# Linear attention and an ELU feed-forward on one core: nine neighbouring tokens per partition for q, whole slots of k and v in the first batch, and feed-forward columns written in token order

## The chip, the cores and the metric

The kernel runs on one core of one Trainium2 chip. The metric is the device time of one execution in microseconds (us). The engines are PE (TensorE, matmuls), DVE (VectorE), ACT (ScalarE), POOL (GpSimd) and SP (SyncE, which here only issues transfers). They run side by side and wait for each other through semaphores.

## What is computed

For each of 8 batches and 8 heads, with 576 tokens and 64 channels: q is normalised by a softmax over its channels, k by a softmax over the tokens, `kv` is a 64x64 matrix per head, and the attention output is `q_s @ kv`. The heads side by side give 4608 rows of 512, which go through a feed-forward network of width 2048 with an ELU between.

```python
q_s = softmax(q, axis=-1)                 # over 64 channels
k_s = softmax(k, axis=2)                  # over 576 tokens
kv  = einsum('bhsd,bhde->...', k_s, v)    # [b, h, 64, 64]
x   = (q_s @ kv).transpose(0, 2, 1, 3).reshape(4608, 512)
h   = x @ w_in                            # [4608, 2048]
g   = where(h > 0, h, exp(min(h, 0)) - 1)
out = g @ w_out                           # [4608, 512]
```

All inputs and the output are float32; q, k and v are 9.4 MB each, the two weights 4.2 MB each.

## The kernel before

A batch's 576 tokens are split into 512 (`SM`, four rows `R` on each of 128 partitions) and a rest of 64 (`SR`). The feed-forward of batch `j` runs in 16 steps (`NCH`), one per 128 columns of the hidden layer. A step has four matmuls into one PSUM bank (`hidden`, line 778), an exponential on ACT (766), a `min`-like step on POOL (767) and the combination on DVE (`elu`, 789), which writes the hidden tile GT. Three steps later (`LAG`) four matmuls (`project`, 799) multiply that GT tile by `w_out` and accumulate in four output banks. The rests of all 8 batches are kept in XTR and go through the network as a ninth round of 16 steps at the end.

While batch `j` is in the feed-forward, the attention of batch `j + 1` is prepared by the same engines. The order is written out by hand in tables of words: `FIRST` for the steps of batch 0, `SECOND` for batch 1, `LATER` for the others. Each step has three strings: words that come after the hidden matmuls, after the project matmuls, and after the elu. `do` turns each word into instructions. The first batch has its own list, `START`, since nothing runs beside it, and `AT` gives its PSUM banks.

The words that matter:

- `load`: transfers of q, k or v, issued on SP's queue in the order of the words. A, B and M are the first four heads, the last four, or all, for the 512 tokens; R is the rest, in two transfers of 64 partitions. `w1` and `w2` load weights on POOL's queue. `hold` lets SP wait for the last hidden matmul.
- `qmax`, `qsub`, `qexp`, `qsum`, `qmul`: softmax of q, into QS (and `qmulr` for the rest, into QSR). A suffix names the engine, with gp for POOL.
- `turn` and `wide`: a DMA transpose of QS into QW and a copy into QT, where channels lie on partitions; `pturn` and `pwide` do it with PE instead.
- `kmax`, `kturn`, `kacross`, `diag`, `kspread`, `copy`: the maximum of k over tokens, for batches 0 and 1. `peak`, `join`, `kout`, `kin` do the same for later batches with a transposing reduction and a small transfer through memory. Then `ksub`, `kexp`; `kraw`, `kmin` do the subtraction with PE in the first batch.
- `vconv`, `kv`, `kfac`: v in bfloat16, the kv matmuls and their normalisation into MB.
- `att` and `xc`, or `flat` and `xflat`: the matmul of MB and QT, and the copy into XT, the input of the feed-forward. `rest0`, `rcopy0` and `xrest` serve the rest.

An engine carries out its instructions in the order of the program. Where an instruction waits, all behind it on that engine waits too. The elu and the store of the output read:

```python
self.op("dve", lambda: v.scalar_tensor_tensor(self.GT[n % NG][:, :], ps, 0.0, ES[:, :],
                                              ALU.max, ALU.min),
...
rows = self.out[j * S:j * S + SM, :].rearrange("(p r) c -> r p c", r=R)[t]
```

Of the kernel before, what the change touches and what calls it, by code (L numbers as in the profile page):

```python
# [17 lines left out]
SR = S - SM  # L18
CUTS = (0, 320, 832, 1344, 1856, 2304)
# [15 lines left out]
AT = {"rawA": 0, "rawA2": 1, "rawB": 3, "rawB2": 2, "rawS": 7, "rawT": 4,  # L35
      "kturnA": 5, "kturnB": 3, "kvA": 5, "kvB": 6, "pturnA": 6, "pturnB": 4,
      "att0": 5, "att1": 7, "att2": 3, "att3": 6}
START = ("load:K:0:A load:Q:0:A load:K:0:R kmax:A qmax:A load:K:0:B kmax:S kraw:A load:Q:0:B kraw:S "
         "kmax:B kmax:T qsub:A:gp qmax:3 warm:4:3 kturn:A load:K:1:R kacross:A load:V:0:A w1:2:4 "
         "w1:0:2 qexp:A kturn:B load:V:0:R diag:act:A w2:0:2 kmin:S kacross:B kexp:S kraw:T w1:4:6 "  # L40
         "qsub:3:gp vconv:R:gp qmax:2 qsum:A diag:dve:B qsub:2:gp qmul:A:dve qexp:3 w2:2:5 kmin:A "
         "qsum:3 load:V:0:B qexp:2 kraw:B kmin:T pturn:A w1:6:8 vconv:A:gp qmul:3:gp kexp:A "
         "load:K:1:M pwide:A:act await:sp:QS0 qsum:2 kv:A kfac:A:dve kmin:B att:0 qmul:2:gp "
         "load:Q:1:A kexp:T att:1 w1:8:10 load:Q:0:R vconv:B:dve pturn:B kexp:B xc:0 kv:B xc:1:dve "
         "kfac:B:dve w2:5:6 load:Q:1:R h:2:4 pwide:B:act att:2 att:3 xc:2 h:0:2 kmax2:B w1:10:12 "
         "xc:3 kmax2:A kmax2:R ")
FIRST = {
    0: ("", "", ""),
    1: ("", "", ""),
    2: ("qmax:A", "w2:6:8", ""),  # L50
    3: ("qsub:0 w1:12:14", "qsub:1:dve", ""),
    4: ("", "qmax0:R qexp:A w2:8:12", "qsum:A load:Q:1:B qsub0:R"),
    5: ("", "kturn kacross", "qexp0:R qmul:A qsum0:R"),
    6: ("diag", "qmax:C", ""),
    7: ("qsub:D:dve", "kspread qsub:2 w1:14:16", "hold copy load:V:1:RAB"),
    8: ("qexp:C", "qmulr0:gp ksub:1:dve", "ksub:0:dve load:K:2:MR"),
    9: ("pturn:A", "ksub:3 ksub:R", "qsum:C pwide:A:act"),
    10: ("qmul:B:dve pturn0:R kexp:A", "pwide0:R:act", ""),
    11: ("vconv:A:dve", "rest0 w2:12:13 vconv:R", "ksub:2:dve rcopy0:act"),
    12: ("load:Q:2:ABR pturn:B kexp:R vconv:B:gp", "", "load:V:2:MR pwide:B:act"),  # L60
    13: ("kv:A", "kexp:B kfac:A:dve att:0", "xc:0 w2:13:15 w2:15:16 peak2:A"),
    14: ("kv:B kfac:B:dve", "att:1 qmulr:dve peak2:B", "xc:1"),
    15: ("peak2:R join2 att:3 xc:3", "", "turn:R att:2 xc:2 kout2"),
}
SECOND = {
    0: ("qmax:A", "qsub:0:dve qmax:C", "load:Q:2:MR qsub:1"),
    1: ("qexp:A", "qsub:D", ""),
    2: ("qsub:2", "", ""),
    3: ("kin qsum:A", "qmul:0", "qexp:C wide0:R:act"),
    4: ("", "qsum:C", "qmul:1:dve ksub:2:dve"),  # L70
    5: ("", "load:K:2:MR", ""),
    6: ("qmulr:dve ksub:R:dve", "kexp:R qmul:B:dve", "ksub:3:dve"),
    7: ("rest0 turn:A", "rcopy0:dve", "vconv:B"),
    8: ("", "vconv:R ksub:A", "kexp:B peak2:B"),
    9: ("peak2:R kexp:A", "vconv:A:dve", "turn:R peak2:A"),
    10: ("", "", "turn:B join2"),
    11: ("", "kv:AB", "wide:A:gp"),
    12: ("kfac:AB:dve", "load:K:3:MR wide:R:act", ""),
    13: ("wide:B:gp", "flat:0", "xflat:0:act"),
    14: ("flat:1", "load:V:2:MR xflat:1:dve flat:2", "xflat:2:act"),  # L80
    15: ("kout2 flat:3", "xflat:3:dve", "flat:4 xflat:4:act xrest:act qmax2:A"),
}
LATER = {
    0: ("qsub:0", "", ""),
    1: ("", "kin qsub:1:dve", "vconv:R"),
    2: ("qsub:2", "", ""),
    3: ("qexp:A", "ksub:R:dve ksub:0:dve", "qsum:A"),
    4: ("", "", "qsub:D ksub:1:dve"),
    5: ("", "ksub:3:dve ksub:2:dve", "qexp:C"),
    6: ("", "kexp:A qmul:A:dve", "qsum:C"),  # L90
    7: ("kexp:B", "vconv:A:gp", ""),
    8: ("vconv:B turn:A kexp:R", "qmulr:gp", ""),
    9: ("", "peak2:A kv:AB qmul:B kfac:AB:dve", "wide:A:act peak2:R"),
    10: ("", "", "load:K:3:MR"),
    11: ("flat:0 xflat:0:act turn:R", "wide:R:act", "qmax2:A"),
    12: ("peak2:B join2", "turn:B", "flat:1 xflat:1:act wide:B:gp"),
    13: ("load:Q:3:MR", "flat:2", "qmax2:C xflat:2:act"),
    14: ("", "flat:3", "load:V:2:MR kout2 xflat:3:act"),
    15: ("flat:4", "", "xflat:4:act xrest:dve"),
}  # L100
CHANGED = {
    0: ("", "", "qmax:C qsub:0"),
    2: ("", "", "qsub:2 load:Q:2:MR"),
}
TABLES = {0: FIRST, 1: SECOND, 2: {**LATER, **CHANGED}}
NONE = ("", "", "")


class Ev:

    __slots__ = ("sem", "val", "know")

    def __init__(self, sem, val, know):
        self.sem, self.val, self.know = sem, val, know


class Gen:
# [103 lines left out]
    def init(self):  # L221
# [8 lines left out]
        for f in range(4):  # L230
            op("gp", lambda: g.memset(self.MB[f][:, :, :].bitcast(F32), 0.0), (), [f"MB{f}"])
# [803 lines left out]
```

## Time and profile before

| | us |
|---|---|
| runs shown (2) | 313.07 and 314.11, median 313.59 |
| profiled execution, whole | 312.28 |
| its span in the profile | 310.5 |
| PE, DVE, ACT, POOL busy | 296.0, 243.8, 177.9, 174.0 |
| elu: each of 144 on DVE | 0.679 |
| subtraction in k, 128x512, on DVE / POOL | 0.745 / 1.727 |
| q's multiply, 128x1024, on DVE / POOL | 1.215 / 1.906 |
| transfers | 51.63 MB, mean 166 GB/s |

The span runs from the first to the last instruction that the profile shows; about 1.8 us of the profiled execution lie around it. Busy times are of one execution. In group lines, the columns are line, engine, operation, output and input tile, shapes, count, then the busy time in us and the mean of one in ns, then the idle time before them and what ended it. An instruction can start before the one ahead of it has quite ended, so sums of means are slightly above the busy time of a window.

### The profile page before, as it was taken

Reading aid. Unit: us, or ns where it says so; the run is one execution under the profiler, and the core shown is the slowest. Engines: PE = TensorE matmul, PEld = TensorE weight load, DVE = VectorE, ACT = ScalarE, POOL = GpSimd, SP = SyncE. Lnnn points to the kernel's source line nnn. Section 1 sums busy time; section 2 is a strip of 40 time slices with the busy share of each in tenths; the row PEclk is TensorE's granted clock in tenths of the full one; section 3 lists DMA queues with packets and bytes.
Section 4 is the critical chain, followed back from the end, with each engine's and each line's share of the span. In section 5 each row is a group of like instructions: output and inputs, shape, how many; then the busy total and the mean of one; then the engine's idle time right before and its main releaser. Section 6 shows DMA issues by size and latency. Waiting matters only on the chain.

```text
span 310.5 us, 4547 instructions
## 1 busy us (share of the span) xinstructions
PE 296.0 (95%) x1601; PEld 236.0 (76%) x1601; DVE 243.8 (79%) x420; ACT 177.9 (57%) x295; POOL 174.0 (56%) x229
## 2 busy tenths in 40 slices
PE   3688999999999999999999999999999999999995
PEld 1356876688778868887887888888888888888884
DVE  6999998999879997999799979997895354335541
ACT  1475786558357845694478556955695543334432
POOL 2987985655636843675467636763676333333330
PEclk9999999999999999999999999999999999999999
DMA  7999999998918695439742974152412030003003
GB/s 234 320 352 328 373 338 312 294 320 146 290 41 246 165 255 167 170 60 268 208 170 48 266 223 169 34 129 70 169 34 44 0 137 0 0 2 136 0 1 135
DMA packets 65607, 51.63 MB, mean 166 GB/s; under 512 B 29360, under 2 KB 58288, under 8 KB 65584
## 3 DMA queue, kind: packets, MB, share of 16 engines
q1 hardware_dynamic: 57984, 41.23, 49.4%
q0 software_dynamic: 6400, 8.39, 10.0%
q10 hardware_dynamic: 1200, 1.72, 1.8%
q8 instruction: 12, 0.20, 0.3%
q14 instruction: 11, 0.09, 0.1%
HBM read 38.27 MB, written 9.45 MB: 154 GB/s over the span
## 4 chain that ended last, share of the span: by engine, by line
PE 80%; DMA 8%; DVE 6%; ACT 2%; POOL 1%; SPq 1%; issue 1%; DVEq 0%
PE bank L778 38%; PE bank L799 38%; DMA QWR<-QSR 4%; DMA W2S<-in_moe_w_out_dram 3%; PE bank L709 2%; DMA KR<-in_k_dram 2%; DVE QZ L604 1%; ACT ES L766 1%; PE bank L535 1%; POOL ES L767 1%; DVE GT L789 1%; DVE QS L618 1%; SPq L276 1%; PE bank L652 1%; DVE KA L299 0%
## 5 line engine op out<-in xcount | busy, mean ns | idle before, releaser
L767 POOL TENSOR_SCALAR ES<-ES 128x512 f32<-128x512 f32 x144 | 95.7, 666 | 119.2 <-ACT ES L766 118.8
L799 PE MATMUL bank<-W2S,GT 128*128 128x512 f32 x576 | 154.5, 392 | 1.2 <-DVE GT L789 0.9
L778 PE MATMUL bank<-XT,W1S 128*128 128x512 f32 x512 | 139.2, 394 | 0.2 <-ACT XT L696 0.2
L789 DVE SCALAR_TENSOR_TENSOR GT<-bank,ES 128x512 fp32r<-128x512 f32 x144 | 96.8, 679 | 50.9 <-PE bank L778 42.0
L766 ACT ACTIVATE ES<-bank 128x512 f32<-128x512 f32 x144 | 85.6, 597 | 87.2 <-PE bank L778 86.4
L799 PEld LDWEIGHTS bank<-W2S,GT 128*128 128x128 f32 x576 | 107.2, 188 | 24.0 <-DVE GT L789 1.4
L778 PEld LDWEIGHTS bank<-XT,W1S 128*128 128x128 f32 x512 | 94.1, 188 | 19.7 <-ACT XT L696 0.9
L594 POOL TENSOR_TENSOR QR<-QR,QM 128x512 f32<-128x512 f32 (+3 forms) x24 | 28.7, 1199 | 5.4 <-DVE QM L586 5.2
L600 ACT ACTIVATE QR<-QR 128x1024 f32<-128x1024 f32 (+3 forms) x18 | 19.0, 1060 | 11.6 <-POOL QR L594 10.2
L586 DVE TENSOR_REDUCE QM<-QR 128x16 f32<-128x1024 f32 (+3 forms) x18 | 21.7, 1208 | 0.5 <-DMA QR<-in_q_dram 0.5
L604 DVE TENSOR_REDUCE QZ<-QR 128x16 f32<-128x1024 f32 (+3 forms) x18 | 21.7, 1206 | 0.0
L731 ACT ACTIVATE XT<-bank 128x512 fp32r<-128x512 f32 (+2 forms) x28 | 15.4, 552 | 10.1 <-PE bank L709 9.9
L414 DVE TENSOR_TENSOR KR<-KR,NB 128x512 f32<-128x512 f32 x25 | 17.8, 745 | 0.3
L778 PE MATMUL bank<-XTR,W1S 128*128 128x512 f32 x64 | 16.6, 389 | 0.0
L452 ACT ACTIVATE EK<-KR 128x1024 bf16<-128x1024 f32 x14 | 14.7, 1050 | 0.8 <-POOL KR L414 0.8
L618 POOL TENSOR_TENSOR QS<-QR,QI 128x1024 f16<-128x1024 f32 (+1 forms) x9 | 14.5, 1617 | 1.1 <-DVE QI L606 1.1
L367 DVE TRANSPOSE_TENSOR_REDUCE KM<-KR 128x32 f32<-128x1024 f32 x12 | 14.8, 1237 | 0.4 <-DMA KR<-in_k_dram 0.4
L778 PEld LDWEIGHTS bank<-XTR,W1S 128*128 128x128 f32 x64 | 12.0, 188 | 2.5
L709 PE MATMUL bank<-QT,MB 128*128 128x320 f32 (+5 forms) x48 | 11.8, 306 | 0.8 <-ACT QT L731 0.7
L709 PEld LDWEIGHTS bank<-QT,MB 128*128 128x128 f32 x48 | 8.5, 188 | 5.0 <-ACT QT L731 1.7
L618 DVE TENSOR_TENSOR QS<-QR,QI 128x1024 f16<-128x1024 f32 (+1 forms) x9 | 10.5, 1170 | 0.1
L809 DVE COPY OSB<-bank 128x512 f32<-128x512 f32 x16 | 10.3, 686 | 0.4 <-PE bank L799 0.3
(96 smaller groups left out, 204.9 us busy)
## 6 DMA issues: line engine op xcount, KB each, us to landing
out_dram<-OSB SPq DMA_DIRECT2D x35, 256.0 KB, 2.8
KR<-in_k_dram SPq DMA_DIRECT2D x7, 1024.0 KB, 6.0
VR<-in_v_dram SPq DMA_DIRECT2D x6, 1024.0 KB, 7.4
QR<-in_q_dram SPq DMA_DIRECT2D x5, 1024.0 KB, 7.2
W1S<-in_moe_w_in_dram POOLq DMA_DIRECT2D x8, 512.0 KB, 11.3
QR<-in_q_dram SPq DMA_DIRECT2D x6, 512.0 KB, 8.2
VR<-in_v_dram SPq DMA_DIRECT2D x4, 512.0 KB, 7.7
W2S<-in_moe_w_out_dram POOLq DMA_DIRECT2D x3, 512.0 KB, 10.4
```

The source lines that it names most:

```text
L414: self.op(en, lambda: e.tensor_tensor(kv, kv, m, ALU.subtract), keys + ["NB"], keys)
L586: self.op("dve", lambda: v.tensor_reduce(self.QM[:, g], QR[:, g, :], AX.X, ALU.max), self.qkeys(b, part), self.qstat("QM", part))
L594: self.op(en, lambda: e.tensor_tensor(QR[:, g, :], QR[:, g, :], m, ALU.subtract), keys + self.qstat("QM", part), keys)
L600: self.op("act", lambda: a.activation(QR[:, g, :], QR[:, g, :], AF.Exp), keys, keys)
L604: self.op("dve", lambda: v.tensor_reduce(self.QZ[:, g], QR[:, g, :], AX.X, ALU.add), self.qkeys(b, part), self.qstat("QZ", part))
L618: self.op(en, lambda: e.tensor_tensor(out, src, z, ALU.mult), keys + self.qstat("QI", part), [f"QS{x}" for x in cells])
L709: last = pe.matmul(self.bank[bank][:, a - c0:b - c0], self.MB[f][:, :, :].rearrange("p u d -> p (u d)"), self.QT[:, f, a - f * S:b - f * S ...
L766: self.op("act", lambda: a.activation(ES[:, :], ps, AF.Exp), [f"bank{bank}"], [ek])
L767: self.op("gp", lambda: g.tensor_scalar(ES[:, :], ES[:, :], -1.0, 1.0, ALU.add, ALU.mult), [ek], [ek])
L778: return pe.matmul(ps, self.W1S[:, kc, c * 128:(c + 1) * 128], x[:, kc, 0:SM], start=(kc == 0), stop=(kc == 3))
L789: self.op("dve", lambda: v.scalar_tensor_tensor(self.GT[n % NG][:, :], ps, 0.0, ES[:, :], ALU.max, ALU.min), [f"bank{bank}", ek], [f"GT{n ...
L799: return pe.matmul(self.bank[OB[t]][:, :], self.GT[n % NG][:, t * 128:(t + 1) * 128], self.W2S[:, c, :], start=(c == 0), stop=(c == NCH - 1))
```

## The change

Three layouts change, and with them the order tables.

- **q**: each partition holds nine neighbouring tokens of four head slots, so the 512 and the rest are one piece. Partitions 0 to 63 hold two heads of a half and 64 to 127 the other two. A batch's q comes in four transfers of 64 partitions with runs of 2304 bytes. The softmax runs on 18 groups of 64 per half. Two DMA transposes of nine blocks replace two of eight and one of two. XT's columns are then ordered by row within the nine first, and by partition second.
- **k and v of the first batch**: loaded as slots of two neighbouring heads, 128 partitions with 2304 bytes in a run. The maximum is one reduction over the nine rows; `kv_first` does 72 matmuls with 64 partitions each, in place of 40.
- **elu and store**: GT is written in token order, which is a step of 8 elements within a row; an output tile then holds 16 groups of 8 neighbouring rows, and its store goes to 16 runs of 16 KB. The ninth round is unchanged in its elu.

For batch 1 the maxima of k are found by `peak` and `join`, so `kturn`, `kspread` and `copy` go. The words of `START`, `FIRST`, `SECOND` and `LATER` are put in a new order, with other engines for some of them.

```diff
-LATER = {
-    3: ("qexp:A", "ksub:R:dve ksub:0:dve", "qsum:A"),
-    5: ("", "ksub:3:dve ksub:2:dve", "qexp:C"),
-    6: ("", "kexp:A qmul:A:dve", "qsum:C"),
...
+LATER = {
+    4: ("ksub:0:dve qexp:B", "ksub:3", "vconv:B"),
+    6: ("qsum:B vconv:A", "ksub:2 qmul:A", "turn:A kexp:R kexp:A"),
+    7: ("", "kexp:B peak2:B", "qmul:B"),
+    9: ("qmax2:A", "vconv:R", "turn:B wide:A:gp"),
...
+START = ("load:K:0:1 load:K:0:0 load:Q:0:1 kmax:A load:Q:0:0 load:K:0:3 qmax:A kraw:A load:K:0:2 "
+         "kraw:T kturn:A qsub:A:gp w1:2:4 load:Q:0:2 load:Q:0:3 kmax:B qmax:2 load:V:0:3 kacross:A "
+         "load:V:0:2 kturn:B qexp:A kacross:B load:Q:1:0 qmax:3 qsub:2:gp diag:dve:A qsub:3:gp "
+         "diag:act:B kraw:B load:V:0:1 kmin:T load:K:1:R load:V:0:0 kraw:S vconv:B:act kmin:A w1:0:2 "
+         "load:K:1:M qexp:2 kmin:B vconv:A:gp kmin:S w2:0:2 qsum:A qmul:A:dve qexp:3 qsum:2 kexp:T "
+         "kexp:A w1:4:7 pturn:A kexp:B w2:2:5 qsum:3 kexp:S kv:A w1:7:10 qmul:3:dve qmul:2:dve kv:B "
+         "pturn:B kfac:A:act pwide:A:act pwide:B:act kfac:B:act att:1 att:0 xc:1 xc:0:dve w1:10:12 "
+         "att:2 h:2:4 xc:2 w2:5:7 att:3 w2:7:10 load:Q:1:1 h:0:2 xc:3 w2:10:13 ")
+FIRST = {
+    0: ("peak:R peak:A hold load:Q:1:2", "peak:B qmax:A", ""),
...
+        if which == "Q":
+            for x in "".join({"A": "01", "B": "23", "M": "0123"}.get(x, x) for x in parts):
+                P, a = int(x) // 2, int(x) % 2
+                dst = t[64 * a:64 * a + 64, 2 * QN * P:2 * QN * (P + 1), :].rearrange("p (u r) d -> p u (r d)", u=2)
+                frm = src[b, 4 * P + 2 * a:4 * P + 2 * a + 2, :, :].rearrange("u (p r) d -> p u (r d)", r=QN)
...
+    def kmax(self, part):
+        v, P = self.E["dve"], "AB".index(part)
+        src = self.KR[0][:, 2 * P * QN:2 * (P + 1) * QN, :].rearrange("p (u r) d -> p u d r", u=2)
+        self.op("dve", lambda: v.tensor_reduce(self.KA[:, 2 * P:2 * P + 2, :], src, AX.X, ALU.max),
...
+            for x in range(2 * P, 2 * P + 2):
+                c0 = VW * (x % 2)
+                for r in range(QN):
+                    for a in range(2):
+                        sl = slice(64 * a, 64 * a + 64)
+                        last = pe.matmul(self.bank[banks[a]][sl, c0:c0 + VW], self.EF[sl, r, x, :],
+                                         self.VF[sl, r, x, :], start=(r == 0), stop=(r == QF))
...
+        ps, out = self.bank[bank][:, :], self.GT[n % NG][:, :]
+        if j < B:
+            ps, ES = (x.rearrange("p (r s) -> p r s", s=QP) for x in (ps, ES))
+            out = out.rearrange("p (s r) -> p r s", s=QP)
+        self.op("dve", lambda: v.scalar_tensor_tensor(out, ps, 0.0, ES, ALU.max, ALU.min),
...
-            rows = self.out[j * S:j * S + SM, :].rearrange("(p r) c -> r p c", r=R)[t]
+            rows = self.out[j * S:(j + 1) * S, :].rearrange("(p r) c -> p r c", r=QN)[
+                16 * t:16 * t + 16, 0:QF, :].rearrange("p r c -> p (r c)")
```

## The prediction

> **What bounds the kernel now.** I read the engine totals and the chain of waits first, then the busy time by stage, then TensorE's timeline, and the DVE groups by shape.
>
> ```profile
> PE 296.0 (95%) x1601; PEld 236.0 (76%) x1601; DVE 243.8 (79%) x420; ACT 177.9 (57%) x295; POOL 174.0 (56%) x229
> ...
> PE 80%; DMA 8%; DVE 6%; ACT 2%; POOL 1%; SPq 1%; issue 1%; DVEq 0%
> ```
>
> The first line gives busy us per engine, the second the shares of the chain. TensorE is the bound, but DVE is only 52 us behind it over the whole span, so the stages matter (columns: length, then busy us and count for PE, PEld, DVE, ACT, POOL; granted clock; DMA share; GB/s):
>
> ```profile
> 25.60:59.80 34.20, 32.78 (x189) 24.70 (x190) 32.92 (x53) 21.96 (x40) 26.23 (x33) 1.00 1.28 332
> 59.80:92.70 32.90, 32.90 (x185) 26.48 (x184) 29.48 (x53) 19.57 (x34) 19.04 (x24) 1.00 0.78 205
> 171.45:202.80 31.35, 31.35 (x183) 25.78 (x177) 28.41 (x49) 20.77 (x34) 18.91 (x24) 1.00 0.59 168
> ```
>
> These are the feed-forward stages of batch 0, of batch 1, and of a later batch. While batch 0 runs, DVE (32.92) is as full as PE (32.78). Later DVE has 3 us of room per batch. The granted clock is 1.00 throughout.
>
> ```profile
> 20.93 1.21 PE L778 MATMUL bank<-XT,W1S 128*128 128x512 f32 x4
> 26.35 1.20 PE L799 MATMUL bank<-W2S,GT 128*128 128x512 f32 x4 [0.92 <-DVE GT L789]
> 31.02 0.60 PE L328 MATMUL bank<-ID,KA 128*128 128x128 f32 x4
> 31.37 1.17 PE L778 MATMUL bank<-XT,W1S 128*128 128x512 f32 x4
> 35.11 0.40 PE L431 MATMUL bank<-DG,ONES 128*128 128x512 f32 x1
> 35.34 1.09 PE L778 MATMUL bank<-XT,W1S 128*128 128x512 f32 x4
> 56.69 1.20 PE L799 MATMUL bank<-W2S,GT 128*128 128x512 f32 x4 [0.31 <-DMA W2S<-in_moe_w_out_dram]
> 113.81 0.51 PE L709 MATMUL bank<-QT,MB 128*128 128x256 f32 x2 [0.68 <-ACT QT L731]
> ```
>
> In PE's timeline the feed-forward starts at 20.93. Groups of four large matmuls then follow every 0.906 us (171.45 to 202.80 holds 32 of them, 29.0 us of its 31.35). There are 288 groups in all: 261 of the 286 us from 20.93 to PE's end at 307.26. Idle PE after the start is small: 34.20 - 32.78 = 1.4 us in batch 0's stage, 0.68 us at 113.
>
> **The change, part by part.**
>
> *What TensorE must do.* The 288 groups stay. For batch 1 the transposes of k's maxima (L328, 31.37 - 31.02 = 0.35 us) and the spreading matmul (L431, 0.23 us) go: **-0.6 us**. The first batch's attention gets 72 half-height matmuls instead of 40 and four more in the subtraction of the maxima. Ten of the old sort took 0.16 us (17.86 to 18.01 to 18.14), so the 32 more are 0.5 us. The four more, by the 0.4 us of one 128x512 at 13.55, are 1.6 us. These lie beside DVE, which was busy 9.76 of 10 us from 10 to 20; I charge nothing here and keep 2 us for the range.
>
> *The elu writes.* For 128 of the 144 elu steps the output now goes out in steps of 8 elements (32 bytes). Nothing in the trace writes float32 in such a step, so its price is bounded from rows near it:
>
> ```profile
> L789 DVE SCALAR_TENSOR_TENSOR GT<-bank,ES 128x512 fp32r<-128x512 f32 x144 | 96.8, 679 | 50.9 <-PE bank L778 42.0 <-PE bank L799 4.5 <-POOL ES L767 4.1
> L390 DVE TENSOR_REDUCE KQ<-KC 32x16 f32<-32x64 f32 x6 | 1.5, 252 | 0.2
> L733 DVE CAST XTR<-XT 128x256 fp32r<-128x256 f32 x5 | 1.4, 284 | 0.0
> L382 DVE TENSOR_REDUCE KC<-KM 128x16 f32<-128x80 f32 x6 | 1.4, 232 | 0.2
> ```
>
> L733 (third row) writes every second element, and 256 take 284 ns. A packed DVE copy, VB<-VR, takes 684 ns for 1024; with about 150 ns fixed that is 0.52 ns each, so 283 ns for 256. The stepped write cost nothing. L390 *reads* in steps of 64 bytes: 64 elements in 252 ns, while L382 reads 80 in steps of 8 bytes in 232. At 1.04 ns an element (reduces of 1024 and 512: 1210 and 682 ns) L390 should take 215, so the wide step cost 37 ns, about 0.55 ns each. On 512 elements that is +0.28 us. A second cycle per element, 512 x 1.04 = +0.53 us, is the far end. A gain is excluded: the same elements are computed. I take 0, since L733 is the row that writes, and keep 0.28 and 0.53 for the rival.
>
> *DVE besides.* I counted the instructions between elu steps in both programs, each by its row. Batch 0's stage: 35.4 before, 33.8 after (two joins and three maxima more, batch 1's k maxima moved ahead of it, a normalising multiply and q subtractions moved). Batch 1's: 30.6 and 31.4. A later one: 31.0 and 28.7, because two k subtractions (0.745 each) and a q multiply (1.21) go to POOL, and 0.9 for slightly longer pieces comes back. Rows overlap at their ends, so I apply differences to the windows: DVE 31.3, 30.3 and 26.1 beside PE's 32.2, 32.9 and 31.35. Room per elu step: (32.2 - 31.3)/16 = 0.06, 0.16 and 0.33 us. At price 0 nothing is due. POOL rises from 18.9 to about 24 of 31.35 (two subtractions at 1.73, half q's multiply 1.9 to two of 2.1, less a 1.04 cast); ES work queued behind a 2.1 us multiply waits about one step of 1.95, and the project step comes three steps later, which covers it.
>
> *SP's queue.* Per later batch it still holds 16 issues: q has four instead of three, the transposes two instead of three. The stores' runs get longer, but no store is on the chain except the last ones, which keep their size. Zero; if stores held the output tiles, the next eviction 31 us later would show it, and 2.8 us to landing leaves that far.
>
> *The start.* DVE's order was: A's maxima, q's, B's tree (8.47 to 11.25), column maxima, sums, multiply 15.70, kfac 18.6, second half 21.2. By the same rows the new order is: kmax A (1152 elements, 1.34) from 5.0, q max A 6.9 to 8.1, kmax B 8.9 to 10.2, q max 0.7, both column maxima 0.8, q max 0.7, diagonal 0.4 to 1.2, sums 1.45, multiply 1.2, two more sums 1.7, two multiplies 1.4, kfac A and B 1.8, a copy 0.7: 21.0 to 21.8 for the first hidden matmul, where 20.93 was. Then batch 1's maxima (2 x 0.43 + 2 x 1.24) and a q max (1.35) stand ahead of the first elu: 21.4 + 4.7 = 26.1 against 25.60. Kmax reads in steps of 256 bytes; at L390's price it adds 0.6 us each. On POOL, v's conversion now waits for v's last quarter, and the loads of W2 0:2 and W1 4:7 are queued behind it, for which the first project and hidden step 4 wait. Ahead of that quarter go 3.96 MB on SP's queue and 1.05 MB of weights; 5.0 of the 6.59 MB that came in 22 us are in by about 18, an estimate from the rates shown below. **+1.0 us**, from -0.5 to +3.
>
> q arrives in loads of 64 partitions. The rate from 0 to 22 us, in 40 slices:
>
> ```profile
> GB/s 0 0 0 65 177 344 384 385 365 320 266 270 344 333 357 347 301 244 300 338 302 247 307 346 345 352 354 333 341 343 331 346 356 384 358 376 391 354 335 341
> ```
>
> The 266 and 270 begin at 5.5 us, when 1.1 MB had come (k A and q A, 0.52 MB each) and the 64-partition pieces of k follow: 0.59 MB of q at 268 instead of 385 is 0.67 us more, 1.3 for both halves; it is inside the +3. The Trainium skill, "SBUF — State Buffer", section "Door 1: The DMA port swizzle", says a 64-partition transfer reaches half the ports, 196 GB/s at 1 MiB; by that q would cost an estimated 1.5 us per half, 3 in all, and the trace's 268 agrees in direction only.
>
> *Stalls.* The 0.68 us at 113 waited for the third transpose, which goes. The W2S wait (0.31) meets a load issued a step earlier. Of 2.1 us idle I take off **-0.6**; the rest may move.
>
> Sum: -0.6 + 1.0 - 0.6 = -0.2 us on the span of 310.5. The profiled execution took 312.28 in all, the shown median is 313.59; against that I forecast 313.4, and the likeliest case's own range is 309.5 to 317.
>
> **The rivals.**
>
> *DVE becomes the bound (slower).* If the stepped write costs d per elu, batch 0's stage gives 16d - 0.9, batch 1's 16d - 2.6, four later ones 16d - 5.2 each, where positive. It decides from d = 0.06; it passes 2% from d = 0.31. At 0.28: 3.6 + 1.9 = +5.5, 319. At 0.53: 7.6 + 5.9 + 4 x 3.3 = +27, 340. For it speaks L390, against it L733 and the 2.3 us of room that DVE gains in each later batch. The Trainium skill, "Advanced Engine Details and Errata", section "SBUF Cachelines", says that a different 16-byte line at each access pays a penalty and that two hits a line are needed; by that rule every elu write here pays, and no run yet shows how much. Chance 0.39: 0.08 within 2%, 0.15 from 320 to 332, 0.16 beyond.
>
> *The start is late.* Half-partition loads and weights behind v's wait: +3 where +1 was taken, and 2 us of PE's extra matmuls exposed: 317.4. For it: DMA's 1.28 share in batch 0's stage. Against: 2304-byte pieces in place of 1 KB. Chance 0.12.
>
> *The start and all stalls improve.* -0.6, -2.1 and -1.5 of start give 309.4, still within 2%. Over 2% needs 6.3 us, and only the start has them: chance 0.06.
>
> Forecast case 0.43 (with the 309.4 case). Sums: faster 0.06, within 2% 0.43 + 0.08 + 0.12 = 0.63, slower 0.31; 2% is about what a measurement of this kernel can tell from no change. The range 308 to 332 leaves out 0.05 below and 0.16 above.
>
> **What would show it.** Right: GT's row stays near 0.68 us, later batches stay 31.3 us apart, first hidden matmul at 21 to 22.5, no transposes of k's maxima inside batch 0's stage. Wrong: GT's row above 0.9 us and PE waiting for DVE GT in every batch (the DVE rival); PE waiting for W1S or W2S before 35 us (the late start); a feed-forward beginning before 18 (the fast one).

## The result and the profile after

The changed kernel takes 345.79 us (median of 344.26 and 347.32; the kernel before 313.59), a ratio of 1.103 with a 95% interval from 1.096 to 1.110. The profiled execution's span is 342.4 us against 310.5, so 31.9 us are to be found. The prediction was 313.4. Below, times are medians of the runs of one kernel, and a ratio is to the kernel before, run beside it; one run each of e11 and e15 (328.86 and 329.29 us) lay in a slower state and is left out.

The page of the changed kernel, with the same two lines as before, engine totals and shares of the chain:

```profile
PE 308.4 (90%) x1630; PEld 234.3 (68%) x1630; DVE 281.4 (82%) x399; ACT 169.3 (49%) x277; POOL 195.5 (57%) x239
...
PE 41%; DVE 35%; POOL 13%; issue 5%; ACT 2%; DMA 2%; SPq 1%; DVEq 0%
```

DVE has 21 instructions fewer than before and 37.6 us more of busy time (281.4 against 243.8), and its share of the chain went from 6% to 35%. The stages of batch 0, of batch 1 and of a later batch, cut at the first elu of each:

```profile
29.05:67.23 38.18, 31.92 (x184) 23.38 (x185) 36.83 (x59) 18.58 (x32) 22.56 (x26) 1.00 1.25 308
67.23:103.74 36.51, 33.43 (x177) 24.90 (x176) 34.39 (x49) 19.48 (x31) 20.21 (x24) 1.00 0.66 176
176.07:211.53 35.46, 32.61 (x176) 24.93 (x175) 32.31 (x46) 19.16 (x31) 23.19 (x27) 1.00 0.62 154
```

The columns are as in the prediction: the length, then the busy time of PE, PEld, DVE, ACT and POOL. In batches 0 and 1 DVE (36.83 and 34.39) is now fuller than PE (31.92 and 33.43). In the later one DVE is 32.31 where the prediction had 26.1, and PE 2.85 us idle where it had none. There neither engine is full: the chain of waits goes to and fro between DVE, POOL and PE, with the elu as its largest part (15.8%). The groups and the waits name the instruction:

```profile
L773 DVE SCALAR_TENSOR_TENSOR GT<-bank,ES 128x512 fp32r<-128x512 f32 x144 | 156.5, 1102 | 44.6 <-PE bank L759 31.4 <-POOL ES L748 7.5 <-PE bank L782 4.5
```

```profile
PEld bank L759 <- DVE GT L773: 17.3, 23, 1.6
```

One elu takes 1102 ns where it took 679, and that mean still holds the 16 of the ninth round at 691. The second row gives us in total, times and the longest: TensorE's weight loads for `hidden` waited 23 times, 17.3 us in all, for the elu that frees their bank. The start of the feed-forward in PE's timeline (20.93 and 26.35 before):

```profile
24.57 1.20 PE L759 MATMUL bank<-XT,W1S 128*128 128x512 f32 x4
...
30.18 1.19 PE L782 MATMUL bank<-W2S,GT 128*128 128x512 f32 x4 [1.33 <-DVE GT L773]
35.12 1.20 PE L782 MATMUL bank<-W2S,GT 128*128 128x512 f32 x4 [1.01 <-DVE GT L773]
```

So three things are to be explained: dearer elus, a start 3.5 us late, and a rest. The table gives, for four kernels, the first elu of batch 0 and the distance to the first elu of the next batch, read from the starts of the elu rows in DVE's timeline. The last two columns are experiments told below.

| us | before | after | e1, contiguous elu | e16, all mends |
|---|---|---|---|---|
| first elu | 25.60 | 29.05 | 28.84 | 25.72 |
| batch 0 | 34.21 | 38.18 | 37.02 | 35.32 |
| batch 1 | 30.77 | 36.51 | 32.55 | 32.29 |
| batch 2 | 32.57 | 36.19 | 33.02 | 32.15 |
| batch 3 | 31.83 | 36.14 | 33.02 | 31.79 |
| batches 4, 5 | 31.29, 31.29 | 35.46, 35.82 | 32.39, 32.67 | 31.80, 31.80 |
| batch 6 | 31.29 | 33.43 | 31.49 | 31.75 |
| span | 310.5 | 342.4 | 322.6 | 314.2 |

### The profile page after: what moved, and what is told of

Its sections match the earlier page's. It is cut to its first block, busy times and chain, and to the rows that moved or that the text cites. A ratio compares the mean times of both kernels' runs of the same rounds, so it can differ in the third digit from the quotient of the medians.

```text
span 342.4 us, 4563 instructions
## 1 busy us (share of the span) xinstructions
PE 308.4 (90%) x1630; PEld 234.3 (68%) x1630; DVE 281.4 (82%) x399; ACT 169.3 (49%) x277; POOL 195.5 (57%) x239
## 4 chain that ended last, share of the span: by engine, by line
PE 41%; DVE 35%; POOL 13%; issue 5%; ACT 2%; DMA 2%; SPq 1%; DVEq 0%
PE bank L759 20%; PE bank L782 17%; DVE GT L773 16%; POOL ES L748 4%; POOL QS L617 4%; DVE QM L584 4%; POOL QR L591 3%; DVE QZ L602 3%; DMA KR<-in_k_dram 2%; PE bank L689 2%; DVE KM L352 2%; DVE KC L372 2%; DVE MB L558 2%; DVE KR L400 1%; ACT ES L747 1%
## 5 line engine op out<-in xcount | busy, mean ns | idle before, releaser
L773 DVE SCALAR_TENSOR_TENSOR GT<-bank,ES 128x512 fp32r<-128x512 f32 x144 | 156.5, 1102 | 44.6 <-PE bank L759 31.4
L759 PE MATMUL bank<-XT,W1S 128*128 128x512 f32 x512 | 142.6, 399 | 11.4 <-DVE GT L773 7.5
L759 PEld LDWEIGHTS bank<-XT,W1S 128*128 128x128 f32 x512 | 93.5, 188 | 42.2 <-DVE GT L773 17.3
L591 POOL TENSOR_TENSOR QR<-QR,QM 128x576 f32<-128x576 f32 (+3 forms) x25 | 29.8, 1199 | 9.9 <-DVE QM L584 9.9
L617 POOL TENSOR_TENSOR QS<-QR,QI 128x1152 f16<-128x1152 f32 (+1 forms) x14 | 29.9, 2138 | 2.7 <-DVE QI L604 2.7
L597 ACT ACTIVATE QR<-QR 128x1152 f32<-128x1152 f32 (+3 forms) x18 | 18.9, 1055 | 10.9 <-POOL QR L591 10.7
L584 DVE TENSOR_REDUCE QM<-QR 128x18 f32<-128x1152 f32 (+3 forms) x18 | 21.4, 1187 | 1.2 <-DMA QR<-in_q_dram 1.1
L602 DVE TENSOR_REDUCE QZ<-QR 128x18 f32<-128x1152 f32 (+3 forms) x18 | 21.6, 1198 | 0.0
L689 PEld LDWEIGHTS bank<-QT,MB 128*128 128x128 f32 x56 | 10.3, 188 | 12.1 <-DVE MB L558 8.0
L400 POOL TENSOR_TENSOR KR<-KR,NB 128x512 f32<-128x512 f32 x12 | 16.1, 1344 | 0.0
L435 PE MATMUL bank<-KR,ID 128*128 128x512 f32 (+1 forms) x12 | 8.6, 850 | 6.8 <-DMA KR<-in_k_dram 6.8
L714 POOL CAST QT<-QW 128x1152 fp32r<-128x1152 f16 x11 | 12.6, 1147 | 0.0
## 6 DMA issues: line engine op xcount, KB each, us to landing
W2S<-in_moe_w_out_dram POOLq DMA_DIRECT2D x4, 768.0 KB, 15.8
```

Of the source, the lines that this page charges most:

```text
L400: self.op(en, lambda: e.tensor_tensor(kv, kv, m, ALU.subtract), keys + ["NB"], keys)
L584: self.op("dve", lambda: v.tensor_reduce(self.qview(self.QM[:, :], b, part), QR, AX.X, ALU.max), self.qkeys(f"QR{b % 2}", b, part), self.q ...
L591: self.op(en, lambda: e.tensor_tensor(QR, QR, m, ALU.subtract), keys + self.qkeys("QM", b, part), keys)
L602: self.op("dve", lambda: v.tensor_reduce(z, QR, AX.X, ALU.add), self.qkeys(f"QR{b % 2}", b, part), self.qkeys("QZ", b, part))
L617: self.op(en, lambda: e.tensor_tensor(out, QR, z, ALU.mult), reads, keys)
L689: last = pe.matmul(self.bank[bank][:, a - c0:b - c0], self.MB[f][:, :, :].rearrange("p u d -> p (u d)"), self.QT[:, f, a - f * S:b - f * S ...
```

## The experiments

The theory was: the stepped write of the elu costs about 0.47 us each and makes DVE the bound; a smaller rest comes from the start and from the new order of words. The rivals were that the order alone, or the long stores, make the loss.

### What the elu's write costs

**e1: the changed kernel with a contiguous elu.** The stores then go out as two transfers of 64 partitions per tile, in rows of 2 KB.

```diff
-        if j < B:
-            ps, ES = (x.rearrange("p (r s) -> p r s", s=QP) for x in (ps, ES))
-            out = out.rearrange("p (s r) -> p r s", s=QP)
...
```

> The changed kernel, but the elu writes GT in the order of its input, and each output tile goes out in two stores with runs of 2 KB. Theory W (the stepped write is the cost): GT's row falls from 1150 to about 680 ns, later batches stand 31.3 us apart again instead of 35.8, and only the start's 3.8 us are left: 316 to 319 us. Rival P (POOL's longer multiplies and the new tables hold the batches): later batches stay above 34 us apart, 328 us or more. Rival L (the long stores matter): this is slower than W says, and output tiles hold up the copies from PSUM.

Measured: 324.53 us (324.15 to 325.96), ratio 1.038 [1.034, 1.042], span 322.6.

```profile
L770 DVE SCALAR_TENSOR_TENSOR GT<-bank,ES 128x512 fp32r<-128x512 f32 x144 | 97.5, 681 | 70.9 <-PE bank L759 48.8
```

The elu fell to 681 ns as theory W had it, and the step of 8 elements was worth 19.8 of the 31.9 us of span. But 12.1 us stay: the theory's 316 to 319 us was missed, as batches 2 to 5 lie 32.4 to 33.0 us apart and not 31.3. The rivals' numbers (above 34 us apart, 328 us or more) did not come either.

**e2: the kernel before, with the step alone.** Every elu of the 8 batches writes in steps of 8 elements; nothing else is touched.

```diff
+        step = 1 if j == B else 8
...
+            ps, es = (x.rearrange("p (r s) -> p r s", r=step) for x in (ps, es))
+            out = out.rearrange("p (s r) -> p r s", r=step)
...
```

> The kernel before, with the elu alone writing in steps of 8 elements for batches 0 to 7; the rows of the output come in another order, as the stores are as before. Theory W: GT's row rises to about 1150 ns and DVE becomes the bound, since the old tables leave it less room: 16 x 0.47 = 7.5 us on each stage's DVE time, 340 to 346 us. Rival P: without the new tables the step costs under 10 us, below 324.

Measured: 340.14 us, ratio 1.087 [1.083, 1.090], span 338.3, at the near edge of the theory's 340 to 346. The write alone, put into the old kernel, costs 27.8 us of span. That is more than in the changed one, and fits with the other work that DVE has: in a later batch, where the elu is contiguous, DVE is busy 28.4 us in the kernel before and 25.6 in e1.

**e3: the kernel before, with a step of 1, 2, 4, ... 128 elements in batches 0 to 7.**

```diff
+        step = 1 if j == B else 2 ** j
...
```

> The kernel before, the elu writing in steps of 1, 2, 4, 8, 16, 32, 64 and 128 elements in batches 0 to 7 (other order of rows in the output). It measures the price by the step. If any new place costs (rule of lines), step 4 (16 bytes) already pays: above 1000 ns from batch 2 on. If only a step beyond 16 bytes pays: 680 ns for steps 1, 2 and 4, and about 1150 ns from step 8 on, flat. If it grows with distance: step 128 well above 1150.

DVE's timeline, an elu each of batch 1 (step 2), batch 2 (step 4) and batch 3 (step 8):

```profile
72.04 0.68 DVE L794 SCALAR_TENSOR_TENSOR GT<-bank,ES 128x512 fp32r<-128x512 f32 x1
...
104.08 1.08 DVE L794 SCALAR_TENSOR_TENSOR GT<-bank,ES 128x512 fp32r<-128x512 f32 x1
...
142.16 1.14 DVE L794 SCALAR_TENSOR_TENSOR GT<-bank,ES 128x512 fp32r<-128x512 f32 x1
```

The whole took 329.04 us. Step 2 (8 bytes) is free, step 4 (16 bytes) takes 1.08 us, and from there on the price is flat: single rows lie between 0.99 and 1.22 for steps of 8 to 128 elements, 512 bytes at the far end. So the edge lies between 8 and 16 bytes, and the first of the three cases named ahead came.

**e4: which accesses pay.** In the kernel before, one stepped access (8 elements) per batch, the other operands contiguous: ACT's exponential writes ES (batch 1) or reads PSUM (2) in steps; POOL reads and writes ES in steps (3); the elu reads ES (4), reads PSUM (5) or writes GT (6) in steps.

```diff
...
+        ao, ai = {1: (st(es), pl(ps)), 2: (pl(es), st(ps))}.get(j, (es, ps))
+        go, gi = {3: (st(es), st(es))}.get(j, (es, es))
...
+        out, ps, es = {4: (pl(out), pl(ps), st(es)), 5: (pl(out), st(ps), pl(es)),
+                       6: (st(out), pl(ps), pl(es))}.get(j, (out, ps, es))
...
```

> The kernel before, with one stepped access of 8 elements per batch, at a different engine each time, and so other output: batch 1 ACT writes ES stepped, 2 ACT reads PSUM stepped, 3 POOL reads and writes ES stepped, 4 DVE reads ES stepped, 5 DVE reads PSUM stepped, 6 DVE writes GT stepped; 0 and 7 none. If a step costs the memory and not the engine: ACT's 597 ns rises to about 1070 in batch 1, POOL's 666 by 470 or more in batch 3, DVE's 680 to 1150 in 4 and 6. If only DVE's write pays: batch 6 alone. PSUM reads (2 and 5): by the reduce L390 nothing is known; no change under the second theory.

ACT's timeline in batches 1 and 2:

```profile
71.58 1.17 ACT L771 ACTIVATE ES<-bank 128x512 f32<-128x512 f32 x1
...
104.94 0.58 ACT L771 ACTIVATE ES<-bank 128x512 f32<-128x512 f32 x1
```

DVE's in batches 4, 5 and 6:

```profile
171.21 1.14 DVE L799 SCALAR_TENSOR_TENSOR GT<-bank,ES 128x512 fp32r<-128x512 f32 x1
...
206.75 0.68 DVE L799 SCALAR_TENSOR_TENSOR GT<-bank,ES 128x512 fp32r<-128x512 f32 x1
...
238.72 1.15 DVE L799 SCALAR_TENSOR_TENSOR GT<-bank,ES 128x512 fp32r<-128x512 f32 x1
```

The whole took 329.18 us. A stepped SBUF access pays on every engine tried: ACT, writing, 1.17 for 0.58; DVE 1.14 reading and 1.15 writing for 0.68; POOL, which read and wrote in steps at once, 1.15 to 1.30 in 12 of the batch's 16 instructions (up to 1.73 in the others) for 0.62. A stepped PSUM read is free on both engines that read it.

**e5: the token order from PSUM reads.** That suggests a form of the changed kernel which keeps the long stores: ACT's exponential and the elu read the bank in steps of 256 bytes and write ES and GT contiguously.

```diff
...
+            src = ps.rearrange("p (r s) -> p s r", s=QP)
...
-            ps, ES = (x.rearrange("p (r s) -> p r s", s=QP) for x in (ps, ES))
-            out = out.rearrange("p (s r) -> p r s", s=QP)
+            ps = ps.rearrange("p (r s) -> p s r", s=QP)
+            ES, out = (x.rearrange("p (s r) -> p s r", s=QP) for x in (ES, out))
```

> The changed kernel with its long stores kept, and the token order made on the reading side: ACT's exponential and the elu read the PSUM bank in steps of 256 bytes, and write ES and GT contiguously. Theory (only SBUF accesses in steps of 16 bytes or more cost; PSUM reads are free): the elu row falls from 1.10 us to about 0.69, ACT's exponential stays at about 0.60, later batches lie 32 to 33 us apart, and the time is 323 to 326 us, as with the contiguous elu. Rival (a PSUM read in 256-byte steps costs as an SBUF step does): the elu row stays at 1.1 us, the exponential rises to 1.1 too, and the time is 344 us or more. Rival (the long stores cost or save something by themselves): elu row 0.69, but a time more than 2 us from 324.5.

Measured: 325.64 us, ratio 1.046 [1.041, 1.050].

```profile
L777 DVE SCALAR_TENSOR_TENSOR GT<-bank,ES 128x512 fp32r<-128x512 f32 x144 | 97.5, 680 | 71.6 <-PE bank L763 48.2 <-POOL ES L752 17.5 <-PE bank L786 4.5
```

Elu 680 ns, exponential 597. e9 below is e1's program once more: 1.045 [1.040, 1.050]. So e5 equals it: 16 KB runs in the store neither gain nor lose anything that shows beside the spread of e1's program (1.038 and 1.045), and the token order can be had for no more than that.

### The start

**e8: q over 128 partitions.** e1 with q's four transfers per batch over all partitions, each of the same bytes and runs as before.

```diff
-                P, a = int(x) // 2, int(x) % 2
-                dst = t[64 * a:64 * a + 64, 2 * QN * P:2 * QN * (P + 1), :].rearrange("p (u r) d -> p u (r d)", u=2)
...
+                x = int(x)
+                dst = t[:, QN * x:QN * (x + 1), :].rearrange("p r d -> p (r d)")
...
```

> The contiguous-elu form of the changed kernel, with each of q's transfers over 128 partitions in place of 64 (q's heads land in exchanged slots, so each head is multiplied with another head's kv). Theory (half-partition transfers slow the start): the last quarters of k land at 9 us instead of 10.5, the first hidden matmul comes 1 to 1.7 us earlier than 24.6, and the time is 322.5 to 323.5. Rival (the bytes ahead of them on the queue set the landing, not the partitions): landing at 10.3 to 10.7, 324 to 325 us.

The stretch from 6 to 12 us in e1 and then in e8; the last number is the rate of the transfers in GB/s:

```profile
6.00:12.00 6.00, 3.33 (x6) 0.94 (x4) 3.61 (x3) 0.31 (x1) 2.24 (x2) 1.00 1.03 252
```

```profile
6.00:12.00 6.00, 4.71 (x10) 1.73 (x10) 5.42 (x7) 1.32 (x2) 3.40 (x3) 1.00 1.03 382
```

The DMA engines are equally busy (1.03) and move 252 GB/s in one and 382 in the other. DVE's second reduction of k starts at 8.59 instead of 10.24, the first hidden matmul at 21.13 instead of 23.51, the first elu at 25.57 instead of 28.84. With the loads whole, the start of the changed order is as early as the old one. The theory holds, and the gain is larger than the 1 to 1.7 us that it gave. It is clear of the spread: in the changed kernel and the eight others here with 64-partition loads and no other change of `START`, the first elu comes at 28.11 to 29.87 us, in the four with 128 partitions (e8, e12, e14, e16) at 25.57 to 26.22. In e8 a slot of q also comes by one transfer in place of two, so that its maximum waits for one; how much of the gain is due to that was not taken apart (before the maximum of slot 2, at 12.87, DVE of e1 stands idle 0.5 us). The time, 322.31 us, shows less: the span is 2.2 us shorter than e1's (320.4 against 322.6), but the ratio, 1.035 [1.030, 1.040], is not apart from e1's 1.038. The stage of batch 0 became 38.74 us long, for which see e15.

**e7: warming matmuls put back** ahead of the first subtraction, in e1's `START`.

```diff
-         "kraw:T kturn:A qsub:A:gp w1:2:4 load:Q:0:2 load:Q:0:3 kmax:B qmax:2 load:V:0:3 kacross:A "
+         "warm:8:3 kraw:T kturn:A qsub:A:gp w1:2:4 load:Q:0:2 load:Q:0:3 kmax:B qmax:2 load:V:0:3 kacross:A "
```

> The contiguous-elu form of the changed kernel, with eight idle transposes on PE put back ahead of the first subtraction of k's maxima, where the changed order had dropped its warming matmuls. Theory (PE runs the start's first matmuls at half speed because it stood idle): the four matmuls of the subtraction take about 1.9 us instead of 3.62, the first hidden matmul comes about 1.5 us earlier than 24.6, and the time falls by 1 to 2 us, to 322.5-323.5. Rival (the start is held by DVE and the landing of k, PE's speed hidden): first hidden matmul within 0.4 us of before and 324 to 325 us.

Measured: 326.91 us, ratio 1.049 [1.043, 1.055]: no gain. The four matmuls took 1.02 and 1.13 us for two each, instead of 3.62 for four in e1. Yet the first hidden matmul came at 24.95 (23.51 in e1), as TensorE then waited 1.51 us for VB, the converted v, and POOL's conversion had waited 2.0 us for the load of v. e9, e1's program without warming, has this wait too (1.18 us). So PE's speed did not set this start and the theory falls; the rival's own ranges were missed as well, on the late side.

### The later batches

**e6: q's multiplies on DVE.** In e1 the chain of a later batch runs over POOL to a wait of PE for MB:

```profile
175.12 1.26 POOL KR L400
176.38 2.08 POOL QS L617
178.46 0.59 POOL ES L748
179.05 2.08 POOL QS L617
181.13 1.18 POOL ES L748 x2
...
182.43 1.34 DVE QM L584
183.77 0.60 DVE GT L770
...
184.76 0.87 DVE MB L558 x3
185.63 0.04 issue
185.67 0.41 PE bank L689
```

Two multiplies of 2.08 us hold ES, so the elu, so the normalised kv (MB) behind it on DVE. e6 moved them:

```diff
-    6: ("qsum:B vconv:A", "ksub:2 qmul:A", "turn:A kexp:R kexp:A"),
-    7: ("", "kexp:B peak2:B", "qmul:B"),
+    6: ("qsum:B vconv:A", "ksub:2 qmul:A:dve", "turn:A kexp:R kexp:A"),
+    7: ("", "kexp:B peak2:B", "qmul:B:dve"),
```

> The contiguous-elu form of the changed kernel, with both halves of q's multiply in batches 2 and later given to DVE in place of POOL. Theory (POOL's 2.1 us multiplies hold back ES, so the elu, so kfac behind it on DVE): later batches go from 32.4-33 us apart to about 31.5, five of them, so 318 to 321 us against 324.5; the idle time of the elu put down to POOL's ES falls from 15.4 us to below 9. Rival (the new order of words or the transfers hold the later batches, not POOL): 323.5 to 326 us. Rival (DVE, with 2.4 us more per batch, becomes late itself): above 326 us, with the elu waited for by PE.

Measured: 329.64 us, ratio 1.058 [1.055, 1.060], later batches 33.5 to 33.9 us apart. The elu's wait for ES fell from 15.4 to 8.2 us as forecast, and the time rose. PE's wait for MB stayed (1.00 us in place of 0.86), since what was late by POOL was now late by DVE's own queue, and in each later batch PE now waits 0.30 to 0.51 us for the elu besides. This is the second rival, DVE late itself. So e6 shows that giving POOL's load to DVE is no cure, not that POOL's load is harmless. What stayed the same was the distance between MB and its first reader.

**e11: the first reader later.** e1 with `flat:0` and `flat:1` one position later.

```diff
-    11: ("", "peak2:R", "flat:0 xflat:0:act wide:B:gp"),
-    12: ("flat:1", "xflat:1:act", "load:V:2:MR load:Q:3:3"),
+    11: ("", "peak2:R", "wide:B:gp"),
+    12: ("flat:0 xflat:0:act", "", "load:V:2:MR load:Q:3:3 flat:1 xflat:1:act"),
```

> The contiguous-elu form, with the first two attention matmuls of the next batch in batches 2 and later moved one position later each. Theory (TensorE stands 0.87 us per later batch for MB, the normalised kv, and this is the whole excess of a later batch beside 0.2 us of work): later batches go from 32.4-33.0 us to 31.5-32.1 us apart, five of them, and the time is 3 to 5 us below the yardstick. Rival (the delay is passed on to the next attention matmul or the first hidden matmuls of the next batch, for which XT is then late): 32.3 to 33 us apart and the time within 1 us of the yardstick.

Measured: 321.61 us, ratio 1.028 [1.022, 1.034], against 327.5 us and 1.045 [1.040, 1.050] of e1's program beside it (e9). The distances from batch 2 to 5 fell from 32.99, 33.02, 32.40, 32.64 to 32.14, 32.16, 31.52, 31.77, and PE waits for MB in none of them. Batch 6 gained nothing (31.52 and 31.75), so it was four batches and not five: 3.2 us by the profiles.

### Batch 0's stage

**e9: e1's program again**, as a yardstick: 327.5 us (326.02 to 329.48).

> The contiguous-elu form of the changed kernel once more, unchanged, as the yardstick for the three kernels that run beside it. Ratio to before 1.034 to 1.046, the spread between the first look at it (1.038) and the form with the token order made by PSUM reads (1.046).

It is within what was expected. The span of its profile is 325.0 us against 322.6 in e1, and the stage of batch 0 took 38.69 us against 37.02: the same program spreads by 2.4 us, and by 1.7 in this stage. The chain in e9:

```profile
33.20 6.65 DMA kmax_scratch<-KU
...
39.88 6.43 DMA NB<-kmax_scratch
...
46.94 1.75 DVE KR L400
48.69 0.61 DVE GT L770
...
49.34 0.81 PE bank L759 x2
```

The maxima of batch 1, which the old kernel made with PE's transposes and a copy, now go out to memory and come back while the loads run: 13.1 us. DVE's subtraction waits for them, with the elu queued behind it.

**e10: DVE's subtractions one and two steps later**, in e1's `FIRST`.

```diff
-    8: ("ksub:2:dve pwide:A:act", "ksub:0:dve", ""),
-    9: ("ksub:1 qexp:B", "pturn0:R qsum:B ksub:3:dve pwide0:R:act", "load:Q:2:1"),
-    10: ("qmul:B", "", "kexp:A ksub:R"),
-    11: ("rest0", "rcopy0:act kexp:B vconv:R vconv:A:dve", ""),
+    8: ("pwide:A:act", "", ""),
+    9: ("ksub:1 qexp:B", "pturn0:R qsum:B pwide0:R:act", "load:Q:2:1 ksub:2:dve"),
+    10: ("qmul:B", "ksub:0:dve", "ksub:3:dve ksub:R"),
+    11: ("rest0", "rcopy0:act vconv:R vconv:A:dve", "kexp:A kexp:B"),
```

> The contiguous-elu form, with DVE's two subtractions of batch 1's k maxima in batch 0's step 8 moved one and two steps later, and the exponentials of k behind them moved along. Theory (the maxima of batch 1 come back through memory only at 44.9 us, and the subtraction that waits for them holds the elu of step 8 behind it on DVE): TensorE's wait of 1.32 us at 47.98 goes, the stage of batch 0 takes 35.0 to 36.0 us instead of 37.0, and the time is 1 to 2 us below the yardstick. Rival (the normalising of q by POOL, which TensorE's transposes wait for, is just as late): the stage stays within 0.5 us of 37.0 and the time within 0.7 us of the yardstick.

**e12: the same with e8's and e11's edits.**

> Contiguous elu, q's transfers over 128 partitions (q's heads in exchanged slots, as in the run that had this alone), the later subtractions and the later attention matmuls together. Theory (start, batch 0's round trip through memory and kfac in the later batches add up): first elu at 25.6, stage of batch 0 about 36.5, later batches 31.5 to 32.1, time 7 to 9 us below the yardstick, so 315 to 318 us and still 0.5 to 1.5 per cent above before, since TensorE has 0.2 us more work in each batch and gains nothing elsewhere. Rival (gains taken up by the next wait): within 4 us of the yardstick.

**e13 and e14: POOL's subtraction too**, behind q's multiply: e13 on e10, e14 on e12.

```diff
-    9: ("ksub:1 qexp:B", "pturn0:R qsum:B pwide0:R:act", "load:Q:2:1 ksub:2:dve"),
-    10: ("qmul:B", "ksub:0:dve", "ksub:3:dve ksub:R"),
+    9: ("qexp:B", "pturn0:R qsum:B pwide0:R:act", "load:Q:2:1 ksub:2:dve"),
+    10: ("qmul:B ksub:1", "ksub:0:dve", "ksub:3:dve ksub:R"),
```

> The contiguous-elu form, with DVE's subtractions of batch 1's maxima moved later as before, and now POOL's one too, behind q's multiply on POOL. Theory (the maxima come back through memory at 44 to 45 us, and whichever engine has a subtraction queued ahead of other work holds that work): POOL's multiply comes at about 43.5 instead of 46.6, TensorE's wait for QS before its second transposes (0.77 to 2.16 us in the last two forms) falls below 0.3, and the stage of batch 0 goes from 36.9-38.7 to about 35.5 us. Rival (the maxima are merely the last of several equal delays): the wait moves to the kv matmuls or to MB, and the stage stays above 36.5.

> All mends together (contiguous elu, q over 128 partitions with heads exchanged, later attention matmuls, later subtractions on DVE) with POOL's subtraction behind q's multiply as well. Theory: stage of batch 0 from 38.3 to 36, and a ratio to before of 1.00 to 1.01 instead of 1.0135. Rival: a stage above 37.5 and a ratio of 1.01 to 1.018.

| | us | ratio [95%] | stage of batch 0 |
|---|---|---|---|
| e10 | 326.13 | 1.041 [1.039, 1.043] | 36.89 |
| e12 | 317.16 | 1.014 [1.009, 1.018] | 38.31 |
| e13 | 325.83 | 1.041 [1.033, 1.049] | 38.96 |
| e14 | 319.78 | 1.022 [1.016, 1.028] | 39.00 |

e10 is not apart from its yardstick: the wait for the elu at 48 us went, and waits of 0.77 us for POOL's QS and 1.66 for QT came. e12 came within its 315 to 318 us and 10 us below the yardstick, so the gains are not taken up by the next wait, as the rival had it; but its stage of batch 0, 38.31 us, missed the 36.5. In e13 and e14 the theories fell: the stage stayed above 36.5 and 37.5, as the rivals had it, and e14's ratio is above even its rival's. Moved later, the subtractions collided with POOL's multiply, as DVE's and POOL's timelines of e13 show:

```profile
46.68 2.12 POOL L617 TENSOR_TENSOR QS<-QR,QI 128x1152 f16<-128x1152 f32 x1
47.05 3.98 DVE L400 TENSOR_TENSOR KR<-KR,NB 128x512 f32<-128x512 f32 x2
48.76 1.73 POOL L400 TENSOR_TENSOR KR<-KR,NB 128x512 f32<-128x512 f32 x1
```

Two subtractions, 0.68 us each by the median of their row, took 3.98 beside POOL: the first 2.29, until 0.54 us after POOL's multiply had ended, and the second 1.76, until 0.54 us after POOL's own subtraction. So moving words could not tell a late return of the maxima from equally late work on POOL and DVE. The last two runs take the wait away and leave the work.

**e15: no wait for memory.** e1's program, batch 1's k subtracted by a constant tile.

```diff
+        if b == 1:
+            wait = ["ONES"]
+            nm = self.ONES[:, :].bitcast(F32).rearrange("p (h d) -> p h d", d=64)
+            nm = nm[:, 0:1, :].broadcast_to([128, 8, 64])
...
```

> The contiguous-elu form with its first order of words; batch 1's k is subtracted by a constant 1 instead of by its maxima (the quotient of the softmax is the same), so the same subtractions run on the same engines but wait for nothing from memory. The maxima are still found, sent out and brought back. Theory (the return of the maxima at 44 to 45 us holds the subtractions, and they hold what is queued behind them): TensorE's wait for the elu at 48-49 us (1.3 to 2.9 us) goes, the stage of batch 0 takes 35.0 to 36.2 us instead of 37.0 to 38.7, and the time is 1 to 3 us lower than the contiguous form's. Rival (the stage is held by POOL's long multiplies of q and by DVE beside them, and the wait for memory is hidden behind these): stage 36.7 to 38.7 and no change of time within 1 us.

**e16: the same with e8's and e11's edits.**

> Contiguous elu, q over 128 partitions with heads exchanged, later attention matmuls in batches 2 and up, the first order of words for batch 1's subtractions, with the constant 1 in them. Theory: first elu at 25.6 to 26.2, stage of batch 0 about 35.5 instead of 38.3 to 39.0, time 314 to 316 us (ratio 1.003 to 1.010). Rival: stage above 37 and a ratio of 1.012 to 1.022.

In e15 the stage of batch 0 took 34.99 us (37.02 and 38.69 with the wait), in e16 35.32 (38.74 in e8, whose order of subtractions it has): the return through memory is worth 2.0 to 3.7 us there. This is clear of the spread, as the eleven profiles of a contiguous elu that wait for the maxima have 36.89 to 39.01 us in this stage. The whole time shows less of it. e15's, 324.45 us (ratio 1.037 [1.030, 1.044]), shows none, as its profile has 1.2 us of a wait for W2S behind it and a later first elu (29.87). e16 is 316.05 us, ratio 1.008 [1.005, 1.011], where e12, whose subtractions wait for the maxima, has 317.16 and 1.014 [1.009, 1.018]: the intervals just overlap, and e12 has another order of subtractions too. No version tried is faster than the kernel before.

## Why the prediction was wrong

**The elu's write** is the step that failed: "I take 0, since L733 is the row that writes." L733 writes every second float32, 8 bytes apart, and e3 shows that such a step is free and that the price begins at 16 bytes and is flat after. The change steps by 32. L390, the row I set aside, reads in steps of 64 bytes and was on the right side of the edge, but with 64 elements it gave 0.55 ns each, where the elu paid (1.15 - 0.68) / 512 = 0.92. The row nearest in kind (a write) was not nearest in what counts (the step). The range was cut at 332 with the far case, 340, outside it. The count of DVE's other work was right for the later batches: 26.1 us forecast, 25.6 to 26.7 in e1.

The Trainium skill, "Advanced Engine Details and Errata", section "SBUF Cachelines", quoted in the rival, holds: two elements per 16-byte line are free, one pays. The Trainium skill's "SBUF — State Buffer", section "Door 1: The DMA port swizzle", puts the free stride at 4 float32; here 4 cost 1.08 us against 0.68, and the measurement decides.

**The rival "DVE becomes the bound"** had the cause, the dearer elu. With the measured d = 0.47 its formula gives 6.6 + 4.9 + 4 x 2.3 = 20.8 us; e1 against the changed kernel gives 19.8. That the sums agree is in part luck, as the split over batches was wrong. Batch 0 gained 1.2 us in e1 and not 6.6, since the later causes below hold it anyway; batch 1 gained 4.0, batches 2 to 5 gained 3.1 to 3.2 each and not 2.3, and batch 6, which the formula leaves out, 1.9. In the later batches DVE is not full either (32.31 of 35.46 us), so there the elu costs by the waits around it and not as the formula has it. The rival's signs appeared as named: GT's row at 1.10 us, and PE waiting for DVE GT.

**The start** was mis-sized: +1.0 where the first elu came 3.45 us late. The mechanism was named, the half-partition loads, but put at 1.3 us for both halves and inside the +3; e8 gives 3.3, and any kernel here with one form of the loads differs from any with the other by 1.9 to 4.3 us in its first elu. The estimate by the Trainium skill's page cited there, 3 us in all, was the nearer one. K's stepped reduction was mis-sized less: 2.12 us where 1.34 + 0.6 = 1.94 was taken.

**"POOL ... the project step comes three steps later, which covers it"** failed. It looked at the reader of GT alone. What was late was MB, queued behind the elu on DVE and read by PE at once: 0.87 us in each of batches 2 to 5 (e11).

**Batch 1's maxima** were counted as a gain, the 0.6 us of PE's transposes. That they now go through memory in the stage where the transfers are busiest (DMA share 1.25) was not counted at all; e15 and e16 put it at 2 to 3.7 us of that stage, of which the whole time shows less.

**Stalls** (-0.6) and **SP's queue** (zero): the first cannot be told from the rest; e5 beside e9 shows no price of the stores' form.

The parts of the span's 31.9 us, by one profile each, where e1's program alone spreads by 2.4: the step 19.8; e1 to e16 8.4, that is the start's loads, MB's reader and the maxima together; 3.7 us stay open: 1.1 in batch 0, 1.5 in batch 1, 0.5 in each of batches 4 to 6, and -0.4 in batch 2. In batches 4 to 6 of e12, whose distances are e16's, PE has no idle time and the same matmuls as before; why they stand 31.8 us apart and not 31.3 was not settled.

## What to carry to other kernels

In these runs a float32 access in SBUF that steps by 16 bytes or more made an elementwise instruction, by the means, 1.6 to 2.1 times as long (128x512, on DVE, ACT and POOL; 16 to 512 bytes on DVE, 32 on the others); read PSUM in the wanted order instead, and write SBUF in rows. When costing an access by a row of the trace, match the step in bytes before the kind of operation. And when a step is moved, ask not only who reads its result but what is queued behind it on its engine, and how soon that is read: moving load from one busy queue to another (e6) can make it worse, where moving the reader by one position (e11) mends it.

## What the runs showed of the hardware

- A stepped SBUF access: free at 8 bytes, 0.99 to 1.22 us for 0.68 from 16 to 512 bytes (e3, DVE writing); at 32 bytes it also costs DVE reading (1.14 for 0.68), ACT writing (1.17 for 0.58) and POOL doing both (1.15 and more for 0.62, e4); PSUM reads in steps of 32 and 256 bytes cost nothing (e4, e5).
- From 6 to 12 us, where q's loads lie among those of k, v and the weights, the transfers moved 252 GB/s with q over 64 partitions and 382 with q over 128, with equal bytes and runs and at the same DMA busy share (e1, e8).
- A DVE subtraction with both inputs in SBUF takes 0.68 us by the median of its row, but 2.29 beside a POOL multiply of 2.12 and 1.76 beside a POOL subtraction of 1.73 (e13), while the elu, with one input in PSUM, took at most 0.694 in all of e1. This agrees with the Trainium skill, "SBUF — State Buffer", section "SBUF: two separate sides": the two engines lock a shared pair of ports for a whole instruction.
- A 2 KB write to memory and its read back, spread over 128 partitions, took 11.5 to 13.6 us while the loads ran (e1, e12), the writes 5.4 to 7.2 us of it.
